# Three edits to a fused attention, MLP and token-mixing kernel: a copy out of a PSUM bank, a deeper MLP lag, three weight pieces kept

## The chip, the cores and the metric

The kernel runs on one core of a Trainium2 chip. The metric is device time in microseconds (us) for one execution; three executions of the kernel before are shown, and one further execution was profiled. Engines are named as in the profile: PE (TensorE matmul), PEld (its weight loads), DVE (VectorE), ACT (ScalarE), POOL (GpSimd), SP (SyncE, whose queue issues the loads).

## What is computed

Windowed attention over 2 batches of 768 tokens and 8 heads of 64, then a layer-normed MLP with residual, then a rotation by learned angles, a mixing of tokens, and a channel product. Cut to what matters here:

```python
x = attention(q, k, v)                       # [2, 768, 512]
xn = (x - mu) / np.sqrt(var + 1e-06) * g_ln
x = x + np.maximum(xn @ w_ch1, 0.0) @ w_ch2  # 512 -> 2048 -> 512
theta = x @ w_theta
zr, zi = x * np.cos(theta), x * np.sin(theta)
y = np.einsum('ts,bsd->btd', w_tok_r, zr) + np.einsum('ts,bsd->btd', w_tok_i, zi)
u = x + y
out = u + np.maximum(u @ w_ch, 0.0)
```

## The kernel before

Tokens lie in 12 tiles of 128 rows (t = 0 to 5 are batch 0, 6 to 11 batch 1). Every large product is made from two-part operands, a rounded high part ("h") and its remainder ("l"), with three matmuls (hh, hl, lh) in place of one. ACT writes the high part; DVE or POOL subtracts it to get the low part. Weights come from memory as 64-bit words in pieces of 128x512. `load_to` (line 286) loads them through SP into three rotating buffers, and `decode` (line 294) turns one piece into float32 with two ACT and two DVE instructions and a single scratch tile `dec`, so a piece cannot start its second ACT instruction (line 306) before DVE has finished the piece ahead (line 308).

**MLP.** `work` (line 784) is a list of 96 steps n: 4 groups of 4 blocks f of hidden units, and in each group 6 chunks of two token tiles. Step n issues `mlp_h` (line 348): 12 matmuls into a bank `hp` (tag "h", two banks), then `hh` on ACT and `hl` on DVE (lines 361 and 362), in tiles with two buffers. It then issues `mlp_o` (line 371) of step n-1: 6 matmuls `op` that read `hh` and `hl`. PE therefore runs hp(n), op(n-1), hp(n+1), op(n). Decoding and splitting of later weights (`split_w`, line 321) is put in between; near the end `early_steps` (line 505) starts the next stage.

**Token stage.** For each tile t, `flip_x` (line 454) transposes x2[t] and writes it as `xth` (ACT, line 273) and `xtl` (DVE, line 274), tiles with three buffers. `times_theta` (line 460) makes the angles `thm` with 12 matmuls in the one bank of tag "m". `sincos` (line 473) reads them there twice: ACT makes k from them (line 475), rounds it in place (line 476), and DVE subtracts 2 pi k from them (line 477):

```python
nc.scalar.activation(k_, th, AF.Copy, scale=INV_TWO_PI, bias=MAGIC)
nc.scalar.activation(k_, k_, AF.Copy, bias=-MAGIC)
nc.vector.scalar_tensor_tensor(y, k_, -TWO_PI_HI, th, ALU.mult, ALU.add)
```

Two more DVE instructions (lines 478 and 479), three on ACT (481 to 483) and the rotation (487 and 488) follow. POOL then restores x2[t] from `xth` and `xtl` (line 495), after which their buffers are free, and z is split (lines 499 and 500). The next tile's thm may enter bank "m" only after line 477. `tok` (line 557) then accumulates 48 matmuls `acc` (line 533) for tile s from the split token pieces `tokh` and `tokl` (`split_tok`, line 438) in six banks; `add_y` (line 543) adds them to x2 at the end of a batch. The 18 token pieces are decoded once; the three of s = 0 are decoded a second time for batch 1 (the end of `order`, line 284, and `decode_ahead`, line 819), since their tiles come from the rotating tag "tmp".

What stands in which place in each engine's queue is set by a scheduler that takes the program's order as priority and fills in by readiness; each queue runs in order.

Of the kernel before, what the change touches and what calls it, by code (L numbers as in the profile page):

```python
# [8 lines left out]
F32 = mybir.dt.float32  # L9
F32R = mybir.dt.float32r  # L10
BF16 = mybir.dt.bfloat16
I32 = mybir.dt.int32
U32 = mybir.dt.uint32
AF = mybir.ActivationFunctionType
ALU = mybir.AluOpType
PSUM = bass.MemoryType.PSUM

P = 128
# [4 lines left out]
TWO_PI_HI = 6.28125  # L23
TWO_PI_LO = 0.0019353071795864769
INV_TWO_PI = 0.15915494309189535
MAGIC = 12582912.0
PI_CLAMP = 3.1415925
CHUNKS = [[0, 6], [1, 2], [3, 4], [5, 7], [8, 9], [10, 11]]
GROUP = 4
# [3 lines left out]
def kernel(ctx, tc, q, kwin, v, n_pair, g_ln, wall, out):  # L33
    nc = tc.nc
    B, NQ, _, NPAIR, _ = q.shape
# [3 lines left out]
    DM = H * D  # L39
    NF = 4 * DM // P  # L40
    NT = 2 * S // DM
    KD = DM // P
    NTT = B * NQ
    SEQ = [t for ts in CHUNKS for t in ts]
    NCH = len(CHUNKS)
    GROUPS = [range(f, f + GROUP) for f in range(0, NF, GROUP)]
    NGR = len(GROUPS)
# [6 lines left out]
    keep = ctx.enter_context(tc.tile_pool(name="keep", bufs=1))  # L54
# [7 lines left out]
    def ps(tag, shape, name):  # L62
        return bank(tag, shape, name, BANKS[tag])

    zero = keep.tile([P, DM], BF16, name="zero")
    nc.vector.memset(zero, 0.0)

    def spin(tag, name, n):

        o = ps(tag, [P, DM], name)  # L70
# [2 lines left out]

    ident = keep.tile([P, P], F32, name="ident")
    make_identity(nc, ident)
    gbc = keep.tile([P, DM], F32, name="gbc")
    x2all = keep.tile([P, NTT, DM], F32, name="x2all")
    x2 = [x2all[:, t, :] for t in range(NTT)]
    nhalf = keep.tile([P, 1], F32, name="nhalf")
# [28 lines left out]

    bias = [at.tile([P, WIN + P], BF16, name=f"bias{h}") for h in range(H)]

    def make_bias():
# [137 lines left out]

    xn_t = {}

    def layer_norm(t, at=at):

        bn = at.tile([P, 6], F32, tag="bn", name=f"bn{t}", bufs=2)
        mv = at.tile([P, 2], F32, tag="mv", name=f"mv{t}", bufs=2)
        rs = rsall[:, t:t + 1]
        nc.vector.bn_stats(bn, x2[t])
        nc.vector.bn_aggr(mv, bn)  # L260
        xn = at.tile([P, DM], F32, tag="xn", name=f"xn{t}", bufs=3)
        nc.gpsimd.tensor_scalar(xn, x2[t], mv[:, 0:1], None, ALU.subtract)  # L262
        nc.gpsimd.tensor_tensor(xn, xn, gbc, ALU.mult)
        nc.vector.tensor_scalar(rs, mv[:, 1:2], 1.0e-6, None, ALU.add)
        nc.gpsimd.tensor_tensor(rs, rs, nhalf, ALU.pow)
        xn_t[t] = xn
# [14 lines left out]
    NW = 8  # L281
    n_staged, n_decoded = [0], [0]
    first_tok = 2 * NF + KD
    order = [*range(first_tok), *range(n_pieces - KD, n_pieces), *range(first_tok, n_pieces - KD), *range(first_tok, first_tok + NT)]

    def load_to(n):
        while n_staged[0] <= min(n, len(order) - 1):
# [57 lines left out]

    ht_t = {}

    def mlp_h(c, f):
        cn = len(CHUNKS[c]) * P
        xh, xl = xt_t[c]  # L350
        wh, wl = split_t[f][0:2]
        hp = ps("h", [P, cn], f"hp{c}_{f}")
        n = 0
        for kk in range(KD):
            a, al = wh[:, kk * P:(kk + 1) * P], wl[:, kk * P:(kk + 1) * P]
            for l, r in ((a, xh), (a, xl), (al, xh)):
                nc.tensor.matmul(hp, l, r[:, kk, :], start=(n == 0), stop=(n == 3 * KD - 1))  # L357
                n += 1
        hh = act.tile([P, cn], F32R, tag="hh", name=f"hh{c}_{f}", bufs=2)
        hl = act.tile([P, cn], F32R, tag="hl", name=f"hl{c}_{f}", bufs=2)  # L360
        nc.scalar.activation(hh, hp, AF.Relu)  # L361
        nc.vector.scalar_tensor_tensor(hl, hp, 0.0, hh.bitcast(F32), ALU.max, ALU.subtract)  # L362
        ht_t[c, f] = (hh, hl)
# [29 lines left out]
    def tmp(nm):  # L393
        return p2["a"].tile([P, DM], F32, tag="tmp", name=nm, bufs=6)
# [34 lines left out]
    def decode_tok(s):  # L429
        for n in range(NT):  # L430
            i = s * NT + n
            tokw[i] = p2["b"].tile([P, DM], F32, name=f"wt{i}") if s else tmp(f"wt{i}")
            decode(TOK + i, tokw[i])
            yield

# [16 lines left out]
    xf_t = {}  # L452

    def flip_x(t):
        hi = p2["a"].tile([P, KD, P], F32R, tag="xth", name=f"xth{t}", bufs=3)
        lo = p2["a"].tile([P, KD, P], F32R, tag="xtl", name=f"xtl{t}", bufs=3)
        transposed(x2[t], hi, lo, "pt", f"xp2_{t}")
        xf_t[t] = (hi, lo)

# [12 lines left out]

    def sincos(t, th):
        k_, y = tmp(f"k{t}"), tmp(f"y{t}")
        nc.scalar.activation(k_, th, AF.Copy, scale=INV_TWO_PI, bias=MAGIC)
        nc.scalar.activation(k_, k_, AF.Copy, bias=-MAGIC)
        nc.vector.scalar_tensor_tensor(y, k_, -TWO_PI_HI, th, ALU.mult, ALU.add)
        nc.vector.scalar_tensor_tensor(y, k_, -TWO_PI_LO, y, ALU.mult, ALU.add)  # L478
        nc.vector.tensor_scalar(y, y, PI_CLAMP, -PI_CLAMP, ALU.min, ALU.max)
        s_, c_ = tmp(f"s{t}"), tmp(f"c{t}")  # L480
        nc.scalar.activation(s_, y, AF.Sin)
        nc.scalar.activation(c_, y, AF.Sin, scale=0.5)
        nc.scalar.activation(c_, c_, AF.Square, scale=2.0**0.5)
        return c_, s_
# [103 lines left out]
    def general():  # L588
# [67 lines left out]
        def get_w(lo, hi):  # L656
            for i in range(lo, hi):
                w[i] = gm.tile([P, DM], F32, tag="w", name=f"g_w{i}", bufs=2 * NF)
                decode(i, w[i])
# [9 lines left out]
        def product(xt, base, name):  # L669
# [2 lines left out]
                nc.tensor.matmul(mp, xt[:, kk, :], w[base + kk], start=(kk == 0), stop=(kk == KD - 1))  # L672
            return mp

        get_w(0, 2 * NF)
        for t in range(NTT):
            layer_norm(t, gm)
            xt = flip(xn_t.pop(t), f"g_xn{t}")
            op = ps("o", [P, DM], f"g_o{t}")
            for f in range(NF):  # L680
                hp = ps("h", [P, P], f"g_h{t}_{f}")
                for kk in range(KD):
                    nc.tensor.matmul(hp, w[2 * f][:, kk * P:(kk + 1) * P], xt[:, kk, :], start=(kk == 0), stop=(kk == KD - 1))
                ht = gm.tile([P, P], F32, tag="ht", name=f"g_ht{t}_{f}", bufs=2)
                nc.scalar.activation(ht, hp, AF.Relu)
                nc.tensor.matmul(op, ht, w[2 * f + 1], start=(f == 0), stop=(f == NF - 1))
            add_mix(t, op)
# [94 lines left out]
    test_n()  # L782

    work = [(g, c, f) for g, fs in enumerate(GROUPS) for c in range(NCH) for f in fs]
    early = iter(())
    for n, (g, c, f) in enumerate(work):
        if g == 1 and n == NCH * GROUP:
            steps_to(NTT * NPAIR + 20)
            at_es.close()
            p2a_es, p2["a"] = stack(name="p2a", bufs=1, side="right")  # L790
        if n == (NGR - 2) * NCH * GROUP + 2 * NW + 1:
            early = early_steps()
        if c == 0 and f + 2 < GROUP:
            split_w(f + 2)
        if g == 0 and c + 1 < NCH and f == 0:
            steps_to(done_at(c + 1))
        mlp_h(c, f)
        next(early, None)
        if n:
            pg, pc, pf = work[n - 1]  # L800
            mlp_o(pc, pf, GROUPS[pg])
            if pc == NCH - 1 and pf + GROUP < NF:
                split_w(pf + GROUP)
        if g or c > 3:
            decode_to(2 * GROUP * (g + 1) + min(NW, (n % (NCH * GROUP)) // 2 if g else 4 * c - 16 + f))
    for _ in early:
# [10 lines left out]
                pass  # L817

    def decode_ahead(n):
        if n <= NQ:  # L820
            for _ in decode_tok(n % NQ):
                pass

    decode_ahead(1)
# [16 lines left out]
    k_ = 0  # L841
# [59 lines left out]
```

## Time and profile before

| | |
|---|---|
| three executions | 593.61 us median (592.47 to 595.19) |
| the profiled execution | 593.01 us, of which 591.0 us lie between its first and last instruction (span) |
| PE busy | 566.1 us (96%) |
| DVE busy | 362.3 us (61%) |
| ACT busy | 279.1 us (47%) |
| POOL busy | 164.7 us (28%) |
| loads of `raw` pieces | 61 of 512 KB, 3.2 us each to landing |

Busy PE time is the union of overlapping matmuls. A 128x512 matmul is shown as 0.40 us long, and a 128x256 one as 0.28 us, while their starts follow each other at 0.23 and 0.12 us; so a stall is read from the distance of starts. Stages in time: attention with the first MLP group up to about 190 us, the rest of the MLP up to 416 us, the token stage with the channel products up to 586 us.

### The profile page before, as it was taken

The numbers are of one execution on the slowest core, as the hardware profiler recorded it, in microseconds if no ns is written. First come the engines' busy times: TensorE is split into PE (matmuls) and PEld (weight loads), VectorE is DVE, ScalarE is ACT, GpSimd is POOL, SyncE is SP. The second block draws the span as 40 slices with busy tenths as digits, with TensorE's granted clock in tenths as the row PEclk, the third lists the DMA queues.
The fourth block names the chain that finished last, engine by engine and source line by source line (L and its number), as shares of the span: only waits on it lengthen the run. The fifth ranks groups of instructions, "written<-read, shape, count | busy, mean of one in ns | idle before, by whom it ended". The sixth has DMA issues, their size and how long they took to land.

```text
span 591.0 us, 9312 instructions
## 1 busy us (share of the span) xinstructions
PE 566.1 (96%) x3531; PEld 464.7 (79%) x3532; DVE 362.3 (61%) x759; ACT 279.1 (47%) x641; POOL 164.7 (28%) x133
## 2 busy tenths in 40 slices
PE   8999999999989999999999999999999898999996
PEld 3466767676878889989778888889788687888896
DVE  6799998646445832278782524552778869871442
ACT  5877574636224611166652415541567776741110
POOL 1445522222223000030310302250256674930000
PEclk9899999999989999999999999999999998999999
DMA  8866565300001510035461000000334410000112
GB/s 270 291 210 206 176 222 167 124 33 2 2 0 37 190 60 1 1 103 184 149 208 35 1 1 1 1 2 1 106 108 142 138 42 1 1 1 1 71 55 94
DMA packets 18980, 50.75 MB, mean 86 GB/s; under 512 B 2288, under 2 KB 4336, under 8 KB 18928
## 3 DMA queue, kind: packets, MB, share of 16 engines
q1 hardware_dynamic: 18928, 50.08, 25.3%
q8 instruction: 30, 0.49, 0.3%
q14 instruction: 22, 0.18, 0.1%
HBM read 46.93 MB, written 3.15 MB: 85 GB/s over the span
## 4 chain that ended last, share of the span: by engine, by line
PE 31%; DVE 13%; ACT 7%; issue 2%; DMA 2%; DVEq 0%; SPq 0%; ACTq 0%
PE op L381 8%; PE hp L357 8%; PE acc L533 7%; PE ch L579 6%; DVE dec L307 3%; PE thm L469 2%; DVE wt L308 2%; ACT dec L306 2%; DMA raw<-in_wall 2%; DVE y L478 1%; DVE tokl L446 1%; DVE c L487 1%; DVE w L308 1%; ACT wt L302 1%; ACT z L499 1%
## 5 line engine op out<-in xcount | busy, mean ns | idle before, releaser
L357 PE MATMUL hp<-xth,w1l 128*128 128x256 f32 x384 | 109.2, 284 | 0.0
L357 PE MATMUL hp<-xth,w1h 128*128 128x256 f32 x384 | 108.8, 284 | 0.0
L357 PE MATMUL hp<-xtl,w1h 128*128 128x256 f32 x384 | 108.5, 283 | 0.0
L362 DVE SCALAR_TENSOR_TENSOR hl<-hp,hh 128x256 fp32r<-128x256 f32 x96 | 40.3, 420 | 84.6 <-ACT hh L361 84.2
L361 ACT ACTIVATE hh<-hp 128x256 fp32r<-128x256 f32 x96 | 36.4, 379 | 106.2 <-PE hp L357 103.8
L381 PE MATMUL op<-w2h,hl 128*128 128x512 f32 x192 | 77.3, 402 | 3.8 <-DVE hl L362 3.7
L533 PE MATMUL acc<-tokh,z 128*128 128x512 f32 (+1 forms) x320 | 79.7, 337 | 0.0
L381 PE MATMUL op<-w2h,hh 128*128 128x512 f32 x192 | 77.2, 402 | 0.5 <-DVE x2all L369 0.5
L357 PEld LDWEIGHTS hp<-xth,w1h 128*128 128x128 f32 x384 | 72.7, 189 | 6.3 <-issue 2.0
L357 PEld LDWEIGHTS hp<-xtl,w1h 128*128 128x128 f32 x384 | 72.7, 189 | 5.5 <-issue 1.2
L381 PE MATMUL op<-w2l,hh 128*128 128x512 f32 x192 | 76.4, 398 | 0.0
L357 PEld LDWEIGHTS hp<-xth,w1l 128*128 128x128 f32 x384 | 72.9, 190 | 1.8 <-issue 1.7
L533 PEld LDWEIGHTS acc<-tokh,z 128*128 128x128 f32 x320 | 55.3, 189 | 7.2
L203 ACT ACTIVATE e<-e,nm 128x256 f32<-128x256 f32 (+1 forms) x96 | 46.1, 482 | 22.1 <-DVE nm L197 21.2
L329 POOL TENSOR_TENSOR w1l<-w,w1h 128x512 fp32r<-128x512 f32 x16 | 22.6, 1410 | 114.0 <-ACT w1h L328 114.0
L533 PE MATMUL acc<-tokl,z 128*128 128x512 f32 (+1 forms) x160 | 54.0, 338 | 0.0
L381 PEld LDWEIGHTS op<-w2h,hl 128*128 128x128 f32 x192 | 36.2, 189 | 16.6 <-DVE hl L362 8.0
L262 POOL TENSOR_SCALAR xn<-x2all,mv 128x512 f32<-128x512 f32 x12 | 19.5, 1628 | 94.4 <-DVE mv L260 94.4
L197 DVE CUSTOM_DVE_ANT_0 e<-s,bias 128x256 f32<-128x256 f32 (+1 forms) x96 | 35.1, 393 | 15.2 <-PE s L191 14.1
L446 POOL TENSOR_TENSOR tokl<-wt,tokh 128x512 fp32r<-128x512 f32 x18 | 26.8, 1495 | 57.2 <-ACT tokh L445 57.2
L306 ACT ACTIVATE dec<-raw 128x512 int32<-128x512 uint32 x45 | 30.0, 666 | 26.8 <-DVE wt L308 14.0
L369 DVE SCALAR_TENSOR_TENSOR x2all<-op,rsall,x2all 128x512 f32<-128x512 f32 x48 | 34.3, 743 | 10.6 <-PE op L381 10.6
(154 smaller groups left out, 1135.8 us busy)
## 6 DMA issues: line engine op xcount, KB each, us to landing
raw<-in_wall SPq DMA_DIRECT2D x61, 512.0 KB, 3.2
k<-in_kwin SPq DMA_DIRECT2D x10, 512.0 KB, 5.5
q<-in_q SPq DMA_DIRECT2D x12, 256.0 KB, 4.0
vc<-in_v SPq DMA_DIRECT2D x12, 256.0 KB, 3.1
out<-o SPq DMA_DIRECT2D x8, 256.0 KB, 2.0
vw<-in_v SPq DMA_DIRECT2D x10, 192.0 KB, 2.6
out<-o SPq DMA_DIRECT2D x8, 128.0 KB, 1.9
vw<-in_v SPq DMA_DIRECT2D x10, 64.0 KB, 3.1
```

The lines of the kernel that those rows point to most:

```text
L197: nc.vector.tensor_tensor_reduce(out=e[:, j, :], in0=s[j], in1=bias[h][:, b0:b0 + nk], scale=-SCALE, scalar=3.0e38, op0=ALU.add, op1=ALU.m ...
L203: nc.scalar.activation(e[:, j, :], e[:, j, :], AF.Exp, bias=nm[:, h:h + 1], scale=-1.0, accum_out=sm[:, h:h + 1])
L306: nc.scalar.activation(t, r.bitcast(U32)[:, :, 0], AF.Copy, scale=2.0**-29 * (1 - 2.0**-15), bias=-0.4999)
L329: (nc.vector if d and f >= GROUP else nc.gpsimd).tensor_tensor(lo, s, hi.bitcast(F32), ALU.subtract)
L357: nc.tensor.matmul(hp, l, r[:, kk, :], start=(n == 0), stop=(n == 3 * KD - 1))
L361: nc.scalar.activation(hh, hp, AF.Relu)
L362: nc.vector.scalar_tensor_tensor(hl, hp, 0.0, hh.bitcast(F32), ALU.max, ALU.subtract)
L369: nc.vector.scalar_tensor_tensor(x2[t], o, rsall[:, t:t + 1], x2[t], ALU.mult, ALU.add)
L381: nc.tensor.matmul(op_t[c][j], l, r, start=(f == fs[0] and n == 0), stop=(f == fs[-1] and n == 2))
L446: (nc.vector if b else nc.gpsimd).tensor_tensor(lo, src, hi.bitcast(F32), ALU.subtract)
L533: mm = nc.tensor.matmul(o, l[:, dsl], r[:, sl], start=first and not (paired and d % 2), stop=end and not (paired and d % 2 == 0))
L579: nc.tensor.matmul(mp, l[:, kk, es], r, start=(kk == 0 and m == 0), stop=(kk == KD - 1 and m == 2))
```

## The change

`sincos` copies the angles out of their bank with an added ACT instruction, and what read the bank now reads the copy. In steps 26 to 71 `mlp_o` lags by two steps in place of one; every third of these steps puts its `hp` in bank "m", and `hh` and `hl` get three buffers. The three token pieces of s = 0 get tiles of their own, and their second loading and decoding goes. To make room, `xth` and `xtl` have two buffers in place of three, and two tiles of the first stage (`zero`, `gbc`) move to a pool that is closed earlier. The branch `general()`, which does not run for these inputs, gets its own copy of `gbc`.

```diff
-    zero = keep.tile([P, DM], BF16, name="zero")
-    gbc = keep.tile([P, DM], F32, name="gbc")
+    gbc = at.tile([P, DM], F32, name="gbc")
+    zero = at.tile([P, DM], BF16, name="zero")
...
-    order = [*range(first_tok), *range(n_pieces - KD, n_pieces), *range(first_tok, n_pieces - KD), *range(first_tok, first_tok + NT)]
+    order = [*range(first_tok), *range(n_pieces - KD, n_pieces), *range(first_tok, n_pieces - KD)]
...
-    def mlp_h(c, f):
+    def mlp_h(c, f, tag):
...
-        hp = ps("h", [P, cn], f"hp{c}_{f}")
+        hp = ps(tag, [P, cn], f"hp{c}_{f}")
...
-        hh = act.tile([P, cn], F32R, tag="hh", name=f"hh{c}_{f}", bufs=2)
-        hl = act.tile([P, cn], F32R, tag="hl", name=f"hl{c}_{f}", bufs=2)
+        hh = act.tile([P, cn], F32R, tag="hh", name=f"hh{c}_{f}", bufs=3)
+        hl = act.tile([P, cn], F32R, tag="hl", name=f"hl{c}_{f}", bufs=3)
...
-            tokw[i] = p2["b"].tile([P, DM], F32, name=f"wt{i}") if s else tmp(f"wt{i}")
+            tokw[i] = p2["b" if s else "a"].tile([P, DM], F32, name=f"wt{i}")
...
-        hi = p2["a"].tile([P, KD, P], F32R, tag="xth", name=f"xth{t}", bufs=3)
-        lo = p2["a"].tile([P, KD, P], F32R, tag="xtl", name=f"xtl{t}", bufs=3)
+        hi = p2["a"].tile([P, KD, P], F32R, tag="xth", name=f"xth{t}", bufs=2)
+        lo = p2["a"].tile([P, KD, P], F32R, tag="xtl", name=f"xtl{t}", bufs=2)
...
-        nc.scalar.activation(k_, th, AF.Copy, scale=INV_TWO_PI, bias=MAGIC)
+        nc.scalar.activation(y, th, AF.Copy)
+        nc.scalar.activation(k_, y, AF.Copy, scale=INV_TWO_PI, bias=MAGIC)
         nc.scalar.activation(k_, k_, AF.Copy, bias=-MAGIC)
-        nc.vector.scalar_tensor_tensor(y, k_, -TWO_PI_HI, th, ALU.mult, ALU.add)
+        nc.vector.scalar_tensor_tensor(y, k_, -TWO_PI_HI, y, ALU.mult, ALU.add)
...
-        mlp_h(c, f)
+        middle = NCH * GROUP + 2 <= n < (NGR - 1) * NCH * GROUP
+        mlp_h(c, f, "m" if middle and n % 3 == 0 else "h")
         next(early, None)
-        if n:
-            pg, pc, pf = work[n - 1]
+        while done[0] < n - (1 if middle else 0):
+            pg, pc, pf = work[done[0]]
             mlp_o(pc, pf, GROUPS[pg])
             if pc == NCH - 1 and pf + GROUP < NF:
                 split_w(pf + GROUP)
+            done[0] += 1
...
-        if n <= NQ:
-            for _ in decode_tok(n % NQ):
+        if n < NQ:
+            for _ in decode_tok(n):
```

Three places show how the queues change. First PE in step 58 (hp2_10 is its first product), before; `op2_8` belongs to step 56, `hh2_8` and `hl2_8` to the same step:

```order
L357 MATMUL hp2_9_3271<-xth2_1044,w1l9_2976 128x256
L381 MATMUL op2_8_3_3288<-w2h8_2948,hh2_8_3251 128x512
L381 MATMUL op2_8_3_3288<-w2l8_2949,hh2_8_3251 128x512
L381 MATMUL op2_8_3_3288<-w2h8_2948,hl2_8_3252 128x512
L381 MATMUL op2_8_4_3289<-w2h8_2948,hh2_8_3251 128x512
L381 MATMUL op2_8_4_3289<-w2l8_2949,hh2_8_3251 128x512
L381 MATMUL op2_8_4_3289<-w2h8_2948,hl2_8_3252 128x512
L357 MATMUL hp2_10_3296<-xth2_1044,w1h10_3006 128x256
```

The same place of the change:

```order
L356 MATMUL hp2_9_3263<-xth2_1044,w1l9_2993 128x256
L380 MATMUL op1_8_1_3193<-w2h11_3060,hh1_11_3222 128x512
L380 MATMUL op1_8_1_3193<-w2l11_3061,hh1_11_3222 128x512
L380 MATMUL op1_8_1_3193<-w2h11_3060,hl1_11_3223 128x512
L380 MATMUL op1_8_2_3194<-w2h11_3060,hh1_11_3222 128x512
L380 MATMUL op1_8_2_3194<-w2l11_3061,hh1_11_3222 128x512
L380 MATMUL op1_8_2_3194<-w2h11_3060,hl1_11_3223 128x512
L356 MATMUL hp2_10_3288<-xth2_1044,w1h10_3023 128x256
```

Between the same two products PE now runs `op` of step 55 in place of step 56. Second, ACT in the token stage from the write of `xth8` on, before (k7 reads the angles of tile 7; wt and dec are the decoding of token pieces):

```order
L273 ACTIVATE xth8_5001<-xp2_8_5003 128x512
L306 ACTIVATE dec51_5048<-raw51_4918 128x512
L302 ACTIVATE wt16_5052<-raw52_4926 128x512
L475 ACTIVATE k7_5023<-thm7_5010 128x512
L302 ACTIVATE wt17_5060<-raw53_4934 128x512
L476 ACTIVATE k7_5023<-k7_5023 128x512
```

The same place of the change:

```order
L272 ACTIVATE xth8_5008<-xp2_8_5010 128x512
L301 ACTIVATE wt16_5058<-raw52_4933 128x512
L305 ACTIVATE dec52_5060<-raw52_4933 128x512
L474 ACTIVATE y7_5031<-thm7_5017 128x512
L301 ACTIVATE wt17_5064<-raw53_4941 128x512
L475 ACTIVATE k7_5030<-y7_5031 128x512
```

The copy y7 stands where k7 stood, behind `xth8` and two instructions of decoding, and k7 comes two places later. Third, DVE from the rotation of tile 8 to the first instruction of y9, before:

```order
L488 TENSOR_TENSOR s8_5157<-s8_5157,x2all_69 128x512
L307 SCALAR_TENSOR_TENSOR dec36_5173<-wt0_5171,dec36_5173 128x512
L487 SCALAR_TENSOR_TENSOR c8_5158<-c8_5158,x2all_69 128x512
L308 SCALAR_TENSOR_TENSOR wt0_5171<-raw36_5045,dec36_5173 128x512
L307 SCALAR_TENSOR_TENSOR dec37_5179<-wt1_5177,dec37_5179 128x512
L446 TENSOR_TENSOR tokl1_0_0_5238<-wt0_5171,tokh1_0_0_5237 128x512
L308 SCALAR_TENSOR_TENSOR wt1_5177<-raw37_5053,dec37_5179 128x512
L274 TENSOR_TENSOR xtl10_5250<-xp2_10_5251,xth10_5249 128x512
L307 SCALAR_TENSOR_TENSOR dec38_5185<-wt2_5183,dec38_5185 128x512
L446 TENSOR_TENSOR tokl1_0_1_5242<-wt1_5177,tokh1_0_1_5241 128x512
L308 SCALAR_TENSOR_TENSOR wt2_5183<-raw38_5061,dec38_5185 128x512
L477 SCALAR_TENSOR_TENSOR y9_5272<-k9_5271,thm9_5258 128x512
```

The same place of the change:

```order
L488 TENSOR_TENSOR s8_5160<-s8_5160,x2all_66 128x512
L445 TENSOR_TENSOR tokl1_0_0_5223<-wt0_3810,tokh1_0_0_5222 128x512
L487 SCALAR_TENSOR_TENSOR c8_5161<-c8_5161,x2all_66 128x512
L445 TENSOR_TENSOR tokl1_0_1_5227<-wt1_3843,tokh1_0_1_5226 128x512
L445 TENSOR_TENSOR tokl1_0_2_5231<-wt2_3874,tokh1_0_2_5230 128x512
L273 TENSOR_TENSOR xtl10_5235<-xp2_10_5236,xth10_5234 128x512
L548 TENSOR_TENSOR x2all_66<-x2all_66,acc0_0_4686 128x4x128
L477 SCALAR_TENSOR_TENSOR y9_5257<-k9_5256,y9_5257 128x512
```

The six decoding instructions are gone, and the first addition of batch 0's sums stands ahead of y9.

## Rows read from the trace of the kernel before

**Rows 1.** The page: span and busy time by engine.
```profile
span 591.0 us, 9312 instructions
...
PE 566.1 (96%) x3531; PEld 464.7 (79%) x3532; DVE 362.3 (61%) x759; ACT 279.1 (47%) x641; POOL 164.7 (28%) x133
```

**Rows 2.** What PE waited for: us in total, times, longest us.
```profile
PE thm L469 <- DVE y L477: 5.6, 3, 2.8
PE op L381 <- DVE hl L362: 3.7, 6, 1.0
```

**Rows 3.** Stretches of 18 MLP steps (length, busy by engine, clock), and one wait on PE.
```profile
207.71:258.47 50.76, 50.76 (x326) 45.79 (x324) 15.26 (x30) 10.10 (x24) 3.09 (x2) 1.00 0.07 22
258.47:314.34 55.87, 53.07 (x325) 45.20 (x324) 43.70 (x68) 34.23 (x67) 11.70 (x9) 1.00 0.51 170
...
310.47 0.50 PE L381 MATMUL op<-w2h,hl 128*128 128x512 f32 x1 [0.97 <-DVE hl L362]
```

**Rows 4.** ACT's and DVE's instructions in time: start, us, engine, operation, [idle before].
```profile
251.51 0.63 ACT L328 ACTIVATE w1h<-w 128x512 fp32r<-128x512 f32 x1 [2.32 <-PE hp L357]
...
313.14 0.39 ACT L361 ACTIVATE hh<-hp 128x256 fp32r<-128x256 f32 x1 [1.56 <-PE hp L357]
...
310.00 0.41 DVE L362 SCALAR_TENSOR_TENSOR hl<-hp,hh 128x256 fp32r<-128x256 f32 x1
```

**Rows 5.** PE's instructions in time around thm of tiles 6, 8, 10 and 11.
```profile
441.64 0.48 PE L469 MATMUL thm<-thh,xth 128*128 128x512 f32 x1
...
464.78 0.65 PE L272 MATMUL xp<-ident,x2all 128*128 128x128 f32 x4
468.26 0.50 PE L469 MATMUL thm<-thh,xth 128*128 128x512 f32 x1 [2.83 <-DVE y L477]
...
493.79 0.50 PE L469 MATMUL thm<-thh,xth 128*128 128x512 f32 x1 [1.99 <-DVE y L477]
...
494.81 0.63 PE L469 MATMUL thm<-thh,xth 128*128 128x512 f32 x1
...
507.63 0.50 PE L469 MATMUL thm<-thh,xth 128*128 128x512 f32 x1 [0.76 <-DVE y L477]
```

**Rows 6.** Two more stretches, with PE's granted clock behind the engines.
```profile
495.50:497.50 2.00, 2.00 (x6) 1.52 (x6) 2.00 (x5) 1.74 (x4) 1.03 (x1) 0.50 0.00 0
...
510.60:586.50 75.90, 75.74 (x433) 66.10 (x431) 36.61 (x55) 18.63 (x35) 9.96 (x7) 1.00 0.11 40
```

**Rows 7.** ACT's instructions in time in the token stage.
```profile
435.63 0.58 ACT L273 ACTIVATE xth<-xp 128x512 fp32r<-128x512 f32 x1
...
437.80 0.58 ACT L475 ACTIVATE k<-thm 128x512 f32<-128x512 f32 x1
...
465.01 0.58 ACT L475 ACTIVATE k<-thm 128x512 f32<-128x512 f32 x1
...
486.94 0.60 ACT L273 ACTIVATE xth<-xp 128x512 fp32r<-128x512 f32 x1
...
490.52 0.69 ACT L306 ACTIVATE dec<-raw 128x512 int32<-128x512 uint32 x1 [2.98 <-DVE wt L308]
...
491.63 0.58 ACT L475 ACTIVATE k<-thm 128x512 f32<-128x512 f32 x1
```

**Rows 8.** Single lines: count, shortest/median/longest ns, first to last start.
```profile
L477 DVE SCALAR_TENSOR_TENSOR y<-k,thm x12: 670/686/690, 355.7 to 517.9; 128x512 f32<-128x512 f32 x12
...
L478 DVE SCALAR_TENSOR_TENSOR y<-k,y x12: 677/694/1797, 356.4 to 519.1; 128x512 f32<-128x512 f32 x12
```

**Rows 9.** POOL's instructions in time: x2 restored from tiles 4 and 7.
```profile
437.82 1.30 POOL L495 TENSOR_TENSOR x2all<-xth,xtl 128x512 f32<-128x512 f32 x1
...
475.76 1.29 POOL L495 TENSOR_TENSOR x2all<-xth,xtl 128x512 f32<-128x512 f32 x1
```

**Rows 10.** DVE in time: first and last of the six second decodings.
```profile
483.33 0.69 DVE L307 SCALAR_TENSOR_TENSOR dec<-wt,dec 128x512 int32<-128x512 int32 x1 [0.38 <-ACT wt L302]
...
492.45 0.69 DVE L308 SCALAR_TENSOR_TENSOR wt<-raw,dec 128x512 int32<-128x512 int32 x1
```

More of the change, by code (lines that the diff above doesn't have):

```diff
@@ L63, in ps @@
         return bank(tag, shape, name, BANKS[tag])
-    zero = keep.tile([P, DM], BF16, name="zero")
-    nc.vector.memset(zero, 0.0)
     def spin(tag, name, n):
@@ L107 @@
     at_es, at = stack(name="at", bufs=1, side="right")
+    gbc = at.tile([P, DM], F32, name="gbc")
+    zero = at.tile([P, DM], BF16, name="zero")
+    nc.vector.memset(zero, 0.0)
     bias = [at.tile([P, WIN + P], BF16, name=f"bias{h}") for h in range(H)]
@@ L252, with layer_norm @@
     xn_t = {}
-    def layer_norm(t, at=at):
+    def layer_norm(t, at=at, gbc=gbc):
         bn = at.tile([P, 6], F32, tag="bn", name=f"bn{t}", bufs=2)
@@ L673, in product @@
             return mp
+        g_again = gm.tile([P, DM], F32, name="g_again")
+        nc.sync.dma_start(g_again, g_ln.partition_broadcast(P))
         get_w(0, 2 * NF)
         for t in range(NTT):
-            layer_norm(t, gm)
+            layer_norm(t, gm, g_again)
             xt = flip(xn_t.pop(t), f"g_xn{t}")
@@ L784 @@
     work = [(g, c, f) for g, fs in enumerate(GROUPS) for c in range(NCH) for f in fs]
-    early = iter(())
+    early, done = iter(()), [0]
     for n, (g, c, f) in enumerate(work):
```

## The prediction, as put on record before the change ran

> **What bounds the kernel now.** I read the page first. PE is busy for 566.1 of 591.0 us [rows 1], so time can only come from what PE loses, and the list of PE's waits says where: 5.6 us in three waits of thm for line 477, the instruction that last reads bank "m", and 3.7 us in six waits of op for hl [rows 2]. These are the two places at which the change aims. A wait is not the whole loss, since PE also refills its pipe and can lose clock, so I then measured losses as distances between starts.
>
> MLP: 18 steps from 207.71 us take 50.76 us, 2.82 us each; the 18 from 258.47 us take 55.87 us [rows 3]. The second stretch thus loses 5.1 us, and five of the six waits lie in it, the last of 0.97 us until 310.47 us [rows 3]. The sixth is ahead of step 26, where the lag does not change.
>
> Token stage: four transposes and then 12 matmuls of thm come up for every tile. At tile 8 thm starts 3.48 us after its neighbour's transposes (464.78 to 468.26), which themselves need 0.35 us; tiles 10 and 11 waited 1.99 and 0.76 us [rows 5]. With about 0.2 us of refill each that is 3.1 + 2.3 + 0.9 = 6.3 us. After the stall of tile 10 PE's granted clock was 0.50, that is 1.2 GHz, for a stretch [rows 6]; eight matmuls there are shown 0.63 us long and not 0.40 (one of them in [rows 5]), which at 0.2 us each is another 1.5 us. In sum 7.8 us. From 510.6 us on PE is busy for 75.74 of 75.90 us [rows 6], so what PE gains by then is gained at the end.
>
> **The change, part by part.** All sums are against the profiled execution, 593.01 us, which lies 0.6 us under the median; the result is then put on the median.
>
> *The longer lag.* It adds no work. PE's order shows that op now follows one hp more. What it can give depends on who paces that stretch. Between 251.51 and 313.14 us ACT does not once end a wait for PE [rows 4]: the chain of ACT, DVE and loads that decodes 18 pieces there runs by itself, with one hl put between any two pieces, and PE waits for it. If hl arrives at the same times as now, then op gains just the one added hp, 12 matmuls or 1.4 us: that is the lower bound. The upper bound is the whole loss, 5.1 us. Two things lie between. The chain starts on work that a product of PE releases (w1h at 251.51 us [rows 4]), and PE reaches that product 1.4 us earlier, because hp runs ahead. And in the new order the last late hl, which ended at 310.41 us behind a slow decoding instruction [rows 4], stands ahead of it, and at the borders of chunks hl stands ahead of two additions of 0.7 us. PE asks for that hl at 309.5 us now (310.47 less 0.97), with some 3.9 us lost before it; without these, and with one hp more ahead, it would ask at 309.5 - 3.9 + 1.4 = 307.0. The hl ends at 310.4 now; less 1.4 for the earlier start and 1.5 for the order (a slow decoding instruction) it ends at 307.5, some 0.5 us late, and a few hl before it can be as late. With refills I leave 1.6 us of the loss standing and take 3.5 us, nearer the upper bound, because both things between move hl ahead. Three buffers for hh and hl and the bank "m" (free since attention) add no wait; a loss has no mechanism here, since hp never asks for a bank whose hl PE has not needed already.
>
> *The copy.* Twelve more ACT instructions, at the 0.58 us of line 475, which reads the same bank [rows 7]. k now reads a copy in SBUF, and so does line 477. The bank is free after the copy, and no longer after k, k and y (about 0.6 us each, and what stands between them). But the copy is not made at once: in ACT's order it stands where k stood, behind xth of the next tile and two decoding instructions. For tile 8 that place was 465.01 us [rows 7]; a copy there ends at 465.6 us. PE asked at 465.4 (468.26 less 2.83), so nearly all of the 3.1 us would go, if ACT were as early as now.
>
> *Two buffers for xth.* That is what makes it late. xth of tile t must now wait until POOL has restored tile t-2. For tile 4 POOL did so from 437.82 to 439.12 us [rows 9], while xth of tile 6 was written from 435.63 us and k of tile 5 from 437.80 [rows 7]. In the new order they come behind 439.1, about 2 us later, and the added copies put in 0.6 us a tile. For tile 7 POOL ended at 477.05 us [rows 9], so tile 9 meets the same. ACT's round thus arrives at tile 8 about 2 us later than now, and most of what the copy brings there is used up. I take 1 us of the 3.1, with 0 and 3.1 as bounds (below nothing is rival 4), nearer to nothing because the delay of 2 us has its rows and nothing seen takes it back.
>
> *The pieces kept.* Away go three loads of 512 KB on SP, six ACT and six DVE instructions; the six on DVE lie between 483.33 and 493.1 us [rows 10] and have 0.7 us each when nothing stands against them. On ACT one of them waited 2.98 us for DVE, with k of tile 9 right behind it at 491.63 us [rows 7]. Without them the copy of tile 9 comes right behind xth of tile 10, now written from 486.94 to 487.54 us [rows 7]; with 2 us of delay carried over and 0.6 for itself it ends at 490.1, and PE asks at 491.8 (493.79 less 1.99) less the 1 us of above, 490.8. The wait of tile 10 goes, and with it the slow clock: 2.3 + 1.5, of which I take 3.2 (bounds 0 and 3.8). For tile 11 I take nothing of 0.9: PE comes earlier there, and POOL restores tile 9 behind four subtractions for batch 0's sums.
>
> *Moved tiles, and `general()`.* zero and gbc are last used by attention; nothing waits for them afterwards. The branch does not run. Cost nothing.
>
> Sum: 3.5 + 1.0 + 3.2 = 7.7 us. 593.0 - 7.7 = 585.3 us for an execution like the profiled one, **586 us** on the median of 593.6. Next late in the token stage would be the splits of batch 1's pieces on DVE and the additions that free the banks of acc; both get at least 4 us of DVE's time back there (six instructions of 0.7 us), so I cost them nothing.
>
> *A rule weighed.* Line 477 took 670 to 690 ns in all twelve cases, with one operand in PSUM; line 478, with both in SBUF, took 677 to 1797 ns [rows 8]. Line 477 becomes such an instruction. I charged nothing by itself for that beyond the delay above; each of the eight of the token stage could grow by at most 1.1 us, 8.9 us on ACT's and DVE's round. The Trainium skill (SBUF — State Buffer, section "SBUF: two separate sides") says that a Vector instruction with two SBUF inputs and a GpSimd instruction that reads SBUF shut each other out for a whole instruction. By that rule, the growth comes whenever POOL is at work, and the trace's two lines agree.
>
> **Rivals.**
> 1. *The side engines' round takes the place of the bank.* xth waits for POOL, ACT is in order, so copy, k and y of the tile before come later too, and thm waits as long as now. For: the 2 us above. Against: from tile 8 on no decoding stands between. Token gain 0 to 1.5 us, MLP 1.4 to 3.5: 589 to 592 us. Chance 0.17, most of it under 590.6.
> 2. *Everything goes.* 5.1 + 7.8 = 12.9 us, 580.7 us, up to 583.5. Needs hl never late, and copies before PE asks. Chance 0.08.
> 3. *No change to be seen.* hl keeps its times and loses its 1.4 us to other waits, the token stage as in rival 1: 591 to 596.5 us. Also covers that the copy, in its place in the queue, is no earlier than what it replaces. Chance 0.08.
> 4. *Slower.* The wait of xth for POOL comes round with every tile. If it costs 3.5 us each (439.12 less 435.63, above) for tiles 6 to 11 and PE pays it all, that is 21 us in place of 7.8: with 3.5 us from the MLP 9.7 us more than now, 603 us. It decides from where POOL's restoring ends less than about 1.5 us (xth and xtl) before PE asks for thm; at tile 6 there are 2.5 us now (439.12 to 441.64 [rows 5]). The growth of line 477 by up to 8.9 us pushes the same way. Chance 0.05.
>
> My own case, 583.5 to 588.5 us, has 0.62.
>
> **How the numbers follow.** A measurement of this kernel tells about 0.5%, 3 us, from no change: faster is under 590.6, slower over 596.6 us. Faster: 0.62 + 0.08 + 0.14 of rival 1 = 0.84. Within: 0.11. Slower: 0.05. The range leaves out rivals 3 and 4 and the ends of 1 and 2: 581 to 590.5 us.
>
> **What would show it.** In the new profile op waits for hl should fall from 3.7 us to about 2, the stretch of 18 steps behind step 46 from 55.9 to about 52.4 us. thm should wait for the copy, not for y, some 2 to 3 us in all, most at tile 8; the granted clock should stay at full speed near tile 10. ACT should wait for POOL ahead of xth. Of raw pieces 58 and not 61 are loaded. I am wrong if thm's start at tile 8 stays where it was relative to the end of the MLP while tile 10 waits too, if thm waits for xth or xtl (rival 4), or if the 18 steps still take 54 us.

## The result, and the profile after

| | before | changed |
|---|---|---|
| executions side by side | 593.42 us median of 8 (592.47 to 595.3) | 587.91 us median of 8 (585.84 to 590.9) |
| ratio | | 0.9916, 95% interval 0.989 to 0.9942 |
| the profiled execution | 593.01 us, span 591.0 | 586.09 us, span 584.2 |

By the ratio the change is worth 5.0 us (3.4 to 6.5), by the two medians 5.5; forecast were 586 us, a range of 581 to 590.5, and "faster" by the prediction's own bound of 590.6. The page of the changed kernel, where [rows 1] stood before, and the loads:

```profile
span 584.2 us, 9281 instructions
...
PE 560.4 (96%) x3531; PEld 463.2 (79%) x3532; DVE 359.8 (62%) x753; ACT 282.3 (48%) x647; POOL 162.7 (28%) x133
...
raw<-in_wall SPq DMA_DIRECT2D x58, 512.0 KB, 3.2
```

What PE waited for, against [rows 2] (us in total, times, longest):

```profile
PE xp L271 <- DVE xtl L273: 4.4, 2, 2.7
...
PE op L380 <- DVE hl L361: 1.8, 2, 1.0
...
PE thm L468 <- DVE xtl L273: 1.1, 2, 0.5
```

The waits of op for hl went from 3.7 to 1.8 us. Those of thm for line 477, 5.6 us, are gone, but 5.5 us of waits for xtl stand in their place (0.5 before): not the angles' bank but the bank of the transposes `xp` is now late, which the next tile may enter only when xtl has been written from it. Where the time went shows in stretches between the same instructions of PE. First the steps of [rows 3], from hp of step 29 to that of step 47, and on to step 65:

```profile
203.92:254.68 50.76, 50.76 (x325) 45.79 (x324) 16.94 (x34) 10.94 (x25) 3.31 (x3) 1.00 0.09 30
254.68:306.83 52.15, 51.30 (x325) 45.65 (x324) 42.74 (x64) 32.16 (x62) 10.14 (x8) 1.00 0.52 173
```

The first stretch is the same to 0.01 us, the second fell from 55.87 to 52.15: the lag gave **3.7 us**. (Ahead of step 29 the changed kernel has put off one op, 1.4 us of work, which it makes up at step 72; between the two this shifts all starts alike.) Then the token stage from the transposes xp6, ahead of thm5, to xp11, ahead of thm10 (windows: length, PE, PEld, DVE, ACT, POOL busy with counts, granted clock, DMA share, GB/s), before:

```profile
429.73:491.15 61.42, 58.59 (x322) 50.39 (x321) 48.51 (x56) 42.22 (x78) 40.74 (x27) 1.00 0.30 103
```

and changed, with the two waits that lie in it and the clock behind the first:

```profile
423.64:488.11 64.47, 60.11 (x323) 51.64 (x322) 49.93 (x57) 44.80 (x81) 39.11 (x27) 0.97 0.22 74
...
461.29 1.11 PE L271 MATMUL xp<-ident,x2all 128*128 128x128 f32 x4 [2.71 <-DVE xtl L273]
476.48 0.66 PE L271 MATMUL xp<-ident,x2all 128*128 128x128 f32 x4 [1.64 <-DVE xtl L273]
...
461.50:464.50 3.00, 3.00 (x10) 2.36 (x10) 2.80 (x2) 1.69 (x4) 2.99 (x3) 0.50 0.00 0
```

This stretch became 3.05 us longer. Half of that is waiting (PE is without work for 4.36 us in place of 2.83), and half is the slow clock behind the first wait, which makes PE's busy time 1.5 us longer. From xp11 to the end, before and changed:

```profile
491.15:591.04 99.89, 92.44 (x510) 79.81 (x508) 54.28 (x79) 31.16 (x60) 23.82 (x17) 0.98 0.09 33
...
488.11:584.20 96.09, 90.71 (x510) 78.50 (x508) 50.59 (x75) 30.33 (x57) 23.66 (x17) 1.00 0.10 34
```

Here 3.8 us were won at tiles 10 and 11, 2.1 of them waiting and 1.7 the slow clock, which followed the wait of tile 10 only before. So the change's own account is 3.7 - 3.05 + 3.8, about 4.4 us.

The two profiled spans differ by 6.8 us, though. The other 2.4 us lie ahead of step 26, where the change has no part: 0.9 us in the first 25 us and 1.5 us at about 175 us. That second place is behind the same wait of PE, for POOL's xn, in both profiles, 2.23 us before and 2.22 us in the changed one. Only before did the clock fall behind it. Before:

```profile
173.60:177.00 3.40, 3.39 (x13) 3.06 (x14) 1.07 (x2) 0.98 (x2) 0.00 (x0) 0.52 0.00 0
```

Changed:

```profile
173.00:177.00 4.00, 4.00 (x29) 3.63 (x28) 1.02 (x2) 1.21 (x3) 0.00 (x0) 1.00 0.00 0
```

Such stretches at 1.2 GHz come and go from one execution to the next, so differences below are taken from the medians, and places from the waits.

### The profile page after: what moved, and what is told of

Its sections match the earlier page's. It is cut to its first block, busy times and chain, and to the rows that moved or that the text cites. A ratio compares the mean times of both kernels' runs of the same rounds, so it can differ in the third digit from the quotient of the medians.

```text
span 584.2 us, 9281 instructions
## 1 busy us (share of the span) xinstructions
PE 560.4 (96%) x3531; PEld 463.2 (79%) x3532; DVE 359.8 (62%) x753; ACT 282.3 (48%) x647; POOL 162.7 (28%) x133
## 4 chain that ended last, share of the span: by engine, by line
PE 31%; DVE 14%; ACT 7%; issue 2%; POOL 1%; DMA 1%; DVEq 0%; SPq 0%; POOLq 0%; ACTq 0%
PE op L380 8%; PE hp L356 7%; PE acc L533 7%; PE ch L579 6%; DVE dec L306 3%; DVE wt L307 3%; PE thm L468 2%; ACT dec L305 2%; DVE y L478 1%; DVE y L477 1%; DVE w L307 1%; ACT tokh L444 1%; POOL x2all L495 1%; DVE tokl L445 1%; DVE c L487 1%
## 5 line engine op out<-in xcount | busy, mean ns | idle before, releaser
L380 PEld LDWEIGHTS op<-w2h,hh 128*128 128x128 f32 x192 | 36.4, 190 | 5.2 <-ACT dec L305 0.7
L305 ACT ACTIVATE dec<-raw 128x512 int32<-128x512 uint32 x42 | 28.0, 667 | 23.9 <-DVE wt L307 9.2
```

The source lines that it names most:

```text
L305: nc.scalar.activation(t, r.bitcast(U32)[:, :, 0], AF.Copy, scale=2.0**-29 * (1 - 2.0**-15), bias=-0.4999)
L380: nc.tensor.matmul(op_t[c][j], l, r, start=(f == fs[0] and n == 0), stop=(f == fs[-1] and n == 2))
```

## The experiments

### Each part alone

**The lag alone** (the kernel before with all of the diff's lines in `mlp_h` and in the loop over `work`; the core of them):

```diff
-        if n:
-            pg, pc, pf = work[n - 1]
+        while done[0] < n - (1 if middle else 0):
+            pg, pc, pf = work[done[0]]
```

> The kernel before with the longer lag alone (bank "m" for every third hp, three buffers for hh and hl). Theory 1 (what the two traces suggest: the lag is worth 3.7 us, the token edits together 0.7 us, the rest of the profiled difference is slow-clock episodes that come and go): 3.7 us less than before, ratio 0.994, and hl waits of op near 2 us. Theory 2 (the token edits are worth the 4.2 us of the prediction and the lag only what is left of the measured 5.5 us): 1.3 us less, ratio 0.998.

Measured: 589.14 us against 592.53, ratio 0.9933 (0.9906 to 0.9961), 4.0 us; waits of op for hl 1.7 us, and thm's waits for line 477 as before:

```profile
PE thm L469 <- DVE y L477: 5.4, 3, 2.6
...
PE op L381 <- DVE hl L362: 1.7, 2, 1.0
```

**The token edits alone.**

```diff
-        middle = NCH * GROUP + 2 <= n < (NGR - 1) * NCH * GROUP
+        middle = False
```

> The changed kernel with the lag taken out again (op follows one step behind everywhere, hp never in bank "m"), the three token edits left in. Theory 1: 0.7 us less than before, ratio 0.999, with PE waiting for line 273 (xtl) ahead of the transposes in place of the angles' bank. Theory 2: 4.2 us less, ratio 0.993.

Measured: ratio 0.998 (0.9955 to 1.0004), with 4.5 us of waits of xp for xtl. Theory 1 stands in both runs: the lag carries nearly the whole gain, and the three token edits together give about 1.2 us, perhaps nothing. Theory 2's 0.993 lies outside the interval.

**The copy alone.**

```diff
-        nc.scalar.activation(k_, th, AF.Copy, scale=INV_TWO_PI, bias=MAGIC)
+        nc.scalar.activation(y, th, AF.Copy)
+        nc.scalar.activation(k_, y, AF.Copy, scale=INV_TWO_PI, bias=MAGIC)
...
-        nc.vector.scalar_tensor_tensor(y, k_, -TWO_PI_HI, th, ALU.mult, ALU.add)
+        nc.vector.scalar_tensor_tensor(y, k_, -TWO_PI_HI, y, ALU.mult, ALU.add)
```

> The kernel before with the copy of the angles alone (three buffers for xth, second decoding left in). Theory 1 (the copy does free the bank; what takes its gain in the changed kernel is the pair of buffers): thm's waits fall from 5.6 us to under 2.5, 2.5 to 3 us less than before, ratio 0.9955. Rival (the copy sits in ACT's queue where k sat, so it comes as late and brings nothing): thm's waits stay over 4.5 us, within 0.5 us of before.

Measured: 594.48 us, ratio 1.0045 (1.0015 to 1.0075), **2.7 us slower**; neither expectation. thm hardly waits any more, but PE waits as long as before, one bank earlier:

```profile
PE xp L272 <- DVE xtl L274: 4.0, 2, 2.5
...
PE thm L469 <- DVE xtl L274: 1.6, 2, 1.1
...
PE thm L469 <- ACT y L475: 0.7, 2, 0.4
```

There are three xth buffers here, so the pair of buffers isn't needed for this to happen. ACT's instructions in time at tile 6 show what the copy does to its queue:

```profile
451.26 0.58 ACT L475 ACTIVATE y<-thm 128x512 f32<-128x512 f32 x1
451.74 0.67 ACT L302 ACTIVATE wt<-raw 128x512 f32<-128x512 f32 x1
452.31 0.62 ACT L476 ACTIVATE k<-y 128x512 f32<-128x512 f32 x1
454.27 0.67 ACT L306 ACTIVATE dec<-raw 128x512 int32<-128x512 uint32 x1 [1.35 <-DVE wt L308]
454.84 0.62 ACT L477 ACTIVATE k<-k 128x512 f32<-128x512 f32 x1
```

With one instruction more ahead of it, the rounding of k now stands behind a decoding instruction that waits 1.35 us for DVE, and it starts at 454.84 us; before it started at 452.09, although PE was 1.4 us further back there. All that follows for this tile (y, sine and cosine, the rotation, the splits of z) is late by that, and xth and xtl of tile 8 stand behind it in the same queues.

**Two xth buffers alone.**

```diff
-        hi = p2["a"].tile([P, KD, P], F32R, tag="xth", name=f"xth{t}", bufs=3)
-        lo = p2["a"].tile([P, KD, P], F32R, tag="xtl", name=f"xtl{t}", bufs=3)
+        hi = p2["a"].tile([P, KD, P], F32R, tag="xth", name=f"xth{t}", bufs=2)
+        lo = p2["a"].tile([P, KD, P], F32R, tag="xtl", name=f"xtl{t}", bufs=2)
```

> The kernel before with two buffers for xth and xtl in place of three, nothing else. Theory 1 (the wait of xth for POOL's restoring is what costs): PE waits 3 to 5 us for xtl ahead of transposes, some of it in place of the waits for line 477, so 1 to 4 us more than before, ratio 1.002 to 1.007. Rival (two buffers cost nothing): within 0.5 us of before and no wait for xtl over 1 us.

Measured: 595.22 us, ratio 1.0036 (1.0008 to 1.0065), 2.1 us slower. The size is theory 1's, but the place isn't: no wait of the transposes for xtl came, thm's waits for line 477 grew from 5.6 to 7.2 us:

```profile
PE thm L469 <- DVE y L477: 7.2, 5, 2.5
```

### Which edit is to blame

Two theories were left: that the copy itself costs (A), or that the pair of buffers takes what the copy would give (B). The four kernels are the changed one with the copy's lines undone; with `bufs=3` again; with both; and a control.

> The changed kernel without the copy of the angles (k and line 477 read the bank again); lag, kept pieces and two buffers stay. Theory A (formed from the first four runs: around tiles 8 to 10 the round of ACT, DVE and POOL is late as a whole, PE waits for it at whichever bank comes up next, and the copy only adds to the round): 2 to 3 us less than the changed kernel, ratio to before 0.987, with waits of thm for line 477 back but shorter than 5.6 us. Theory B (the pair of xth buffers alone takes the copy's gain, the copy itself does good): waits of thm come on top, 1 to 3 us more than the changed kernel, ratio 0.994 to 0.997.

> The changed kernel with three buffers for xth and xtl again; the room comes from sine and cosine written over k and y, and four scratch tiles in place of six. Copy, lag and kept pieces stay. Theory A: PE still waits for xtl at about the same place as in the copy-only kernel, part of it is gone because the kept pieces are: 1 to 2 us less than the changed kernel, ratio 0.989. Theory B: the wait of the transposes for xtl goes and the copy gives what the prediction wanted: 4 us less than the changed kernel, ratio 0.985.

> As the one with three xth buffers, and without the copy: lag and kept pieces alone are left of the change. Theory A: the best of these, 4 us less than the changed kernel, ratio 0.985, some 2 us under the one with the copy. Theory B: worse than the one with the copy by 2 to 3 us, since thm waits for line 477 at tile 8.

> Control: the changed kernel with only the shared scratch (sine and cosine over k and y, four scratch tiles), two xth buffers. Both theories: within 1 us of the changed kernel, ratio 0.991. If it is off by more, the two kernels before it must be read against this one.

The room for three buffers was made so (the last of the four has these lines alone):

```diff
-        return p2["a"].tile([P, DM], F32, tag="tmp", name=nm, bufs=6)
+        return p2["a"].tile([P, DM], F32, tag="tmp", name=nm, bufs=4)
...
-        s_, c_ = tmp(f"s{t}"), tmp(f"c{t}")
+        s_, c_ = k_, y
```

| run | median us | ratio, interval | waits in the token stage |
|---|---|---|---|
| without the copy | 587.07 | 0.9891 (0.9854 to 0.9928) | thm for y 5.0 |
| three xth, copy | 585.32 | 0.9876 (0.9828 to 0.9924) | xp for xtl 3.0, thm for the copy 1.2 |
| three xth, no copy | 587.54 | 0.9906 (0.9877 to 0.9934) | thm for y 4.3 |
| shared scratch alone | 589.68 | 0.9967 (0.9936 to 0.9998) | xp for xtl 4.3 |

These were inconclusive between A and B. With two buffers the kernel without the copy is some 1.5 us faster than the changed one, as A had it, but less than its 2 to 3; with three buffers the one without the copy, which was to be A's best, came 1.8 us behind the one with it, as B had it. Neither difference is clear of the intervals, so what the copy itself is worth beside the other edits stays open; in the kernel before it costs 2.7 us. The control was off by more than the expected 1 us (about 3), so the two kernels with three buffers are read against it: the third buffer then gives some 5 us beside the copy (the intervals do not meet). The waits do not show these 5 us, 4.2 against 4.3 in the two profiles; what differs there is the clock, which fell to 1.2 GHz twice for 3.4 us between xp6 and xp11 in the control, and not in the other. What the table does show is another thing: whichever buffer is added and whether the copy is there, PE waits 4 to 5.5 us in sum, only the bank changes. So something behind all of the banks must be late.

### The round of the side engines

The chain of waits of the changed kernel, from 455 to 480 us, has no PE in it (start, us, engine and line):

```profile
454.16 1.67 DVE wt L307
455.83 1.15 DVE s L488
...
457.48 0.69 DVE c L487
...
458.23 1.66 POOL x2all L495
459.92 0.60 ACT xth L272
...
461.67 1.70 DVE dec L306
463.39 1.67 DVE wt L307
465.08 0.68 ACT dec L305
465.78 0.56 DVE dec L306
...
467.07 1.70 DVE wt L307
```

Two things are to be seen. xth of tile 8 starts at 459.92 us, when POOL has restored tile 6 (458.23 and 1.65 us more): the pair of buffers does hold it up. But much of the chain is DVE, and its decoding instructions take 1.67 to 1.70 us in place of 0.69. In the stretch from xp6 to xp11, 16 of DVE's 52 two-operand 128x512 instructions take over 0.8 us, 14.3 us above 0.69 in sum; before, 16 of 51 and 13.3 us. By start and duration each of these 16 starts while a POOL instruction is at work. The other two-operand instructions of DVE that meet one in the changed kernel began ahead of it or read one operand from a bank, and take their usual 0.69 us. The Trainium skill (SBUF — State Buffer, section "SBUF: two separate sides") has the rule for it that the prediction weighed for line 477 alone: a Vector instruction with two SBUF inputs and a GpSimd instruction that reads SBUF exclude each other for a whole instruction. The trace agrees with it, at 1.67 to 1.70 in place of 0.69 us. This gave theory C (DVE, stretched beside POOL, is the late engine), tried from both sides.

**Less work for DVE:**

```diff
-        nc.vector.scalar_tensor_tensor(o, r[:, :, 1], -2**31, t, ALU.bitwise_and, ALU.bitwise_or)
+        if not first_tok + NT <= i < first_tok + NT * NQ:
+            nc.vector.scalar_tensor_tensor(o, r[:, :, 1], -2**31, t, ALU.bitwise_and, ALU.bitwise_or)
```

> The changed kernel without the second DVE instruction (line 307) of the 15 token pieces decoded in the token stage: the pieces lack their low bits. Theory C (DVE is the late engine of the round at tiles 7 to 9: decoding, and instructions stretched to 1.6 us and more beside POOL): 12 or more instructions of 0.7 to 1.7 us go ahead of tile 9, the wait of the transposes for xtl (4.4 us) falls under 1 us, 3 to 4 us less than the changed kernel, ratio to before 0.985. Rival (ACT's order or POOL's restoring holds xth up, whatever DVE does): the wait stays over 3 us, within 1 us of the changed kernel.

**Less work for POOL, DVE's as it was:**

```diff
-            (nc.vector if b else nc.gpsimd).tensor_tensor(lo, src, hi.bitcast(F32), ALU.subtract)
+            if b:
+                nc.vector.tensor_tensor(lo, src, hi.bitcast(F32), ALU.subtract)
```

(and `lo` is `hi` for batch 0).

> The changed kernel without POOL's subtractions for batch 0's token pieces (18 of 1.3 to 1.7 us; the high part is read in place of the low one). DVE's own work is unchanged. Theory C: of the 16 DVE instructions between tiles 5 and 10 that take over 0.8 us (14.3 us above 0.69 in sum) less than half are left, DVE's round is 1.5 us a tile shorter, the waits for xtl fall under 1.5 us, 3 to 4 us less than the changed kernel. Rival: as for the run before it, waits over 3 us.

**POOL's work given to DVE** (the changed kernel without the copy, `nc.vector` for every tokl):

```diff
-            (nc.vector if b else nc.gpsimd).tensor_tensor(lo, src, hi.bitcast(F32), ALU.subtract)
+            nc.vector.tensor_tensor(lo, src, hi.bitcast(F32), ALU.subtract)
```

> A version for use: lag and kept pieces, no copy, and batch 0's 18 subtractions for tokl on DVE in place of POOL (0.69 us each, three a tile). Theory C: DVE gets 2.1 us a tile more of work and loses about 1.5 to 2 us of stretching, so the result lies near the kernel without the copy, 586 to 588 us, ratio 0.989; if stretching counts for more than the work, 584 us. Rival (only the number of DVE instructions counts): 3 us more than without the copy, ratio 0.994.

Measured, in the order of the three: 579.18 us, ratio 0.9791 (0.9755 to 0.9827); 578.48 us, 0.9772 (0.9739 to 0.9805); and 579.81 us, **0.9785** (0.9749 to 0.9821). No wait of thm or xp is left on the list of any of them, so the rivals of the first two, waits over 3 us, are out, and so is the third's, that only the number of DVE's instructions counts. All three gained more than theory C expected. The stretch from xp6 to xp11, without the instruction on DVE:

```profile
426.02:484.11 58.09, 58.09 (x322) 50.35 (x321) 39.54 (x46) 42.73 (x78) 35.63 (x26) 1.00 0.18 60
```

without the subtractions on POOL:

```profile
424.05:482.13 58.08, 58.08 (x322) 50.35 (x321) 44.05 (x61) 46.44 (x84) 24.55 (x17) 1.00 0.21 73
```

and with them on DVE:

```profile
429.21:487.30 58.09, 58.09 (x323) 50.35 (x321) 53.48 (x70) 41.68 (x75) 25.29 (x16) 1.00 0.22 78
```

All three take the 58.09 us that PE needs by itself; before it took 61.42 and with the change 64.47. Busy time by count, a DVE instruction takes 0.88 us on average in the changed kernel, 0.72 and 0.76 us in the two with a lighter POOL; without the subtractions 8 of the 16 long ones are left, 6.2 us above 0.69 in sum, about the half that was expected.

The last kernel corrects theory C. DVE has more to do there, not less (busy for 53.48 of 58.09 us, against 49.93 of 64.47), and hardly less stretching: 12 instructions take over 0.8 us, 11.5 us above 0.69 in sum against 14.3. So neither the amount of DVE's work nor the sum of its stretching decides by itself. What differs is which instructions are stretched. In the changed kernel 12 of the 16 meet a subtraction on POOL, and six of these lie on the chain between 454 and 480 us (wt, s, wt, wt, c and y), some 5.8 us above 0.69 in sum. In the last kernel 8 of the 12 are the subtractions themselves, which no engine is seen to wait for, and the chain of the same window is PE alone:

```profile
by line: PE acc L532 71.0%; PE thm L468 25.9%; PE xp L271 3.5%
```

Another reading is that POOL is the late engine, since the restoring of x2 stands behind subtractions in its queue. DVE's rotation (line 487) releases it, and in the changed kernel it starts within 0.1 us of that at tiles 5 to 8; only at tile 4 it comes 1.1 us after it, behind a subtraction (first two rows; the others are tiles 6 and 7):

```profile
430.61 0.69 DVE L487 SCALAR_TENSOR_TENSOR c<-c,x2all 128x512 f32<-128x512 f32 x1 [0.38 <-ACT c L483]
432.43 1.29 POOL L495 TENSOR_TENSOR x2all<-xth,xtl 128x512 f32<-128x512 f32 x1
...
458.23 1.65 POOL L495 TENSOR_TENSOR x2all<-xth,xtl 128x512 f32<-128x512 f32 x1 [1.23 <-DVE c L487]
...
473.59 1.29 POOL L495 TENSOR_TENSOR x2all<-xth,xtl 128x512 f32<-128x512 f32 x1 [0.63 <-DVE c L487]
```

So POOL's queue explains little of it. Each of the three edits also let the scheduler order the queues anew, and no run holds that order fixed; how much of the gain comes from it stays open. The gain, some 7 us against the changed kernel (0.979 to 0.9916), was twice what theory C expected: it reckoned from the waits of xp, while the stretch holds 6.4 us of loss (64.47 less 58.09) with refills and the slow clock. The subtraction itself, on POOL in the changed kernel and on DVE in the last (count, shortest/median/longest ns):

```profile
L445 POOL TENSOR_TENSOR tokl<-wt,tokh x18: 1287/1304/1757, 300.4 to 477.3; 128x512 fp32r<-128x512 f32 x18
```

```profile
L445 DVE TENSOR_TENSOR tokl<-wt,tokh x36: 679/693/1822, 308.2 to 527.8; 128x512 fp32r<-128x512 f32 x36
```

**Are the kept pieces needed then?** The kernel before with the lag and that one line, nothing else:

> The kernel before with the lag and with batch 0's 18 subtractions for tokl on DVE in place of POOL; no copy, no kept pieces, three xth buffers, second decoding left in. Theory C (the stretched round of DVE was the whole loss of the token stage): thm waits under 1 us in all, within 1.5 us of the version with the kept pieces, ratio 0.979 to 0.982. Rival (the second decoding, six DVE instructions at tiles 9 and 10, still makes thm late there): waits of 2 us or more at tiles 10 and 11, ratio 0.984 to 0.986.

Measured: 584.36 us, ratio 0.9828 (0.9785 to 0.9872). The time lies between the two expectations, the waits are the rival's: all up to tile 9 are gone, but behind the second decoding thm is late again, by 0.3 us at tile 10 and 2.4 us at tile 11:

```profile
PE thm L469 <- DVE y L477: 2.7, 2, 2.4
```

So the kept pieces are worth about 2.5 us more (0.9828 less 0.9785; the intervals overlap, and the kernel with them has two xth buffers, not three). No run has them alone. The best version is the lag, the kept pieces and tokl on DVE: 12 to 13 us under the kernel before, 1.3% under the changed kernel.

## Why the prediction came out right

**The lag: right, 3.5 us forecast, 3.7 us in the profile, 4.0 us (2.3 to 5.6) alone.** The 18 steps were to take 52.4 us and took 52.15; the waits for hl were to fall to about 2 us and fell to 1.8. One late hl of 0.81 us is left in these steps, at the place that the prediction named, the end of the chain of decoding:

```profile
302.67 0.50 PE L380 MATMUL op<-w2h,hl 128*128 128x512 f32 x1 [0.81 <-DVE hl L361]
```

**The pieces kept: right in the profile, 3.2 us forecast, 3.8 us found** from xp11 to the end. The wait of tile 10 went, and the clock there stayed at its full level, as forecast. In the profile the 0.9 us of tile 11, which were left standing, are down to 0.5. As 1.7 of the 3.8 us are the slow clock, which does not follow such a wait in every execution, an average execution may gain less; the runs above put the pieces at about 2.5 us.

**The copy: wrong, and this is the step that failed.** "I take 1 us of the 3.1, with 0 and 3.1 as bounds": the stretch with tiles 8 and 9 lost 3.05 us instead (half of it the slow clock), and alone the copy costs 2.7 us. The delay of ACT's round by the pair of buffers was named with its rows and came (ACT waited for POOL ahead of xth twice, 1.7 us in all), but was charged only against the copy's gain. Two effects were not charged: the copy pushes the rounding of k behind a decoding instruction that waits for DVE, and PE's next need, the bank of the transposes, is held by the same late engines. The 2 to 3 us of waits for the copy that were to stay on thm came as 4.4 us on xp, where none of the prediction's signs looked; of thm's waits for xtl, its sign of rival 4, there are 1.1 us and 0.5 before. Behind both stands the late round of DVE and POOL, which the kernel before has already: with part of DVE's decoding or with POOL's subtractions taken out, the waits on both banks are gone. Line 477 itself was costed rightly: with both operands in SBUF it grew once in twelve, by 0.9 us:

```profile
L477 DVE SCALAR_TENSOR_TENSOR y<-k,y x12: 678/684/1600, 350.1 to 513.0; 128x512 f32<-128x512 f32 x12
```

**The rivals.** Rival 1 told the token stage better than the main case did: a side engines' round in place of the bank, with a gain of 0 to 1.5 us there (0.7 found). Its time, from 589 us, was too high because it cut the lag as well. Rival 4 had the mechanism at work, at 3 us and not 21.

**The sum.** 7.7 us were forecast, the change's own account is 4.4, and 5.0 us (3.4 to 6.5) were measured. The forecast of 586 us was near since the lag and the kept pieces carry it. That the time also stayed inside the main case, at 587.91 us of 583.5 to 588.5, is in part luck: the copy's term came out 4 us worse than forecast, more than the 2.5 us that the main case allowed above 586.

## What to carry to other kernels

When PE waits for a bank, look at what is behind the bank before adding a buffer or a copy: here each of them moved the wait to the next bank and left 4 to 5 us of it, because the engines that empty all of the banks were late. Look for instructions on DVE that take twice their usual time beside POOL, and ask which of them lie on the chain: moving 18 subtractions from POOL to the busier engine, DVE, left nearly as many stretched, but others, and gained more (6.3 us by the ratios) than all three token edits. An instruction added to an in-order queue is to be costed by what it pushes behind a waiting one, not by its own 0.58 us.

## What was not expected of the hardware

After PE waits of 1.5 to 2.8 us the granted clock was sometimes at 1.2 GHz for 3 to 4 us (about 1.5 us lost each time) and sometimes not, even behind the same wait of 2.2 us in the same place. Executions of one program differ along with it: in the series with the parts alone, the kernel before took 589.4 us at a mean granted clock of 0.997 and 595.6 us at 0.984. The clock can be low at the start as well: in the profile of the best version it was at 1.2 GHz from 12 to 28 us, though PE was at work there. Why it falls in one execution and not in the next stays open.
